# Attention on one core: negated maxima, 1/8 in the keys' copy, the queries' split off GpSimd, V^T P^T in two bursts

## The chip, the cores and the metric

The kernel runs on one core of a Trainium2 chip. A core has a matrix engine (TensorE, in the profile PE, its weight loads apart as PEld), VectorE (DVE), ScalarE (ACT), GpSimd (POOL) and SyncE (SP), which only issues transfers. The metric is the device time of one execution in microseconds (us). Before the change the median of 3 runs is 1202.78 us (1196.05 to 1207.08).

## What is computed

Attention over 4 batches of 8 heads (576 queries and keys of 64 numbers each, with gates `s` that add up along the keys, causal), then a mixture of 8 experts with two experts a token, then a gated layer:

```python
scores = scale * np.matmul(q, k.transpose(0, 1, 3, 2))          # scale = 1/8
cum = np.cumsum(np.maximum(s, 0.0), axis=-1)
bias = -(cum[:, :, :, None] - cum[:, :, None, :])
scores = np.where(causal, -1000000000.0, scores + np.minimum(bias, 0.0))
scores = scores - np.max(scores, axis=-1, keepdims=True)
attn = np.exp(scores)
attn = attn / (np.sum(attn, axis=-1, keepdims=True) + 1e-09)
x = np.matmul(attn, v)                                          # per head
...                                                             # per token, over its two experts of 8:
out[mask] += top2_w[mask, k, None] * (np.maximum(x[mask] @ w1[e], 0.0) @ w2[e])
...
return (1.0 / (1.0 + np.exp(-(x @ w_gate))) * (x @ w_val)) @ w_out
```

## The kernel before

The change touches attention only, which lies at 12 to 262 us of the program; behind it come the experts (L164 to L260) and the last layer (L490 to L561).

**Tiles and steps.** The 32 heads are handled as 16 pairs, p = 0 to 15; four pairs make a batch. A pair's 576 queries are cut into five tiles of 128 (tile 4 holds the last 64 of both heads), taken in the order of `ORD`, (0, 4, 3, 1, 2). Each (pair, tile) is one step, n = 5p + 0..4, 80 in all. All engines execute their instructions in the order in which the program is written (a manual schedule), and the loop at L1005 to L1026 writes it, step by step: the parts of V^T P^T due at that step (`pre`, from the table `AVS`), then the scores of the step, then its row maxima, then the turned probabilities P^T of the step before last (between its banks the things that `todo` lists for the step), then the exponentials, then what `post` and the rest of `todo` list. `advance` lays in the routing of a finished batch, one instruction or a few at a time.

**Operands.** Scores are computed in two float32r parts: `split(p)` makes them for pair p. A load brings queries `qr` and keys `kr` with the same 64 rows twice over the 128 partitions. Of the queries, `qs` is a rounded copy in all 128 rows (L613 on GpSimd) whose second 64 rows are then replaced by the rest, `qr - qs` (the low part, L628 on GpSimd). For the keys, `kk` is the rounded copy (L611 on ScalarE) and `k2` the low part, a head at a time (L628 on VectorE). `q2` is a copy of the queries' high part by a transfer that SyncE issues (L648). Rows 64 to 67 of `q2` and `k2` hold the cumulative gates, which `sums` makes once, eightfold. For pair 0 all of this stands at the start, with the queries' copy on ScalarE. For pair p the generator `split` is advanced at step 5p - 5 (a piece at its end) and at the three steps after.

**Scores to probabilities.** `scores` (L713 to L715, tile 4: L720 to L723) writes a PSUM tile `sc` of two banks, of which there are two, so the scores of step n + 2 wait for the exponentials of step n. `rowmax` finds the maxima (reductions L732, L735) and multiplies them by -1/8 (L733, L736). `softmax` computes exp(sc / 8 + nm) on ScalarE (L751, L754), and `turn` transposes by PE (L771) into one of three banks, copied out by ScalarE (L611; the end of tile 4 by VectorE, L781).

**V^T P^T.** `av(p, j)` adds key tile j's part for both heads (L800); j = None is all of the first 128 queries', copied by VectorE (L803); after j = 4 ScalarE copies the other 448 (L611). `AVS` lists the steps counted from the pair's first, and the parts that come ahead of that step's scores:

```python
AVS = ((8, (None, 0)), (9, (1,)), (10, (2,)), (11, (3, 4)))
```

**Routing.** Six steps behind a batch its tokens are turned (L825), their logits computed (L840, L848) and routed by a chain of small instructions, most on VectorE (`gate`, L863 to L939), with GpSimd scattering the tokens' rows (L943, L944), five steps of the generator between two tiles of tokens. The last batch's routing runs beside the first expert. At steps 68 to 73 the first expert's first three blocks of weights are split too (copy on ScalarE L145, low part on GpSimd L146).

Of the kernel before, what the change touches and what calls it, by code (L numbers as in the profile page):

```python
# [61 lines left out]
def attn_moe_moe2_kernel(ctx: ExitStack, tc: tile.TileContext, q, k, v, s, wgn, noise, wcat, w2cat, out):  # L62
# [51 lines left out]
    def count():  # L114
        """How many tiles of slots each expert needs beyond those of the static schedule, and the most of any"""
# [23 lines left out]
def weights(nc, stage, pool, wcat, e, f, name="w", lo=None):  # L139
    """A block of an expert's weights in two float32r parts; yields between its load and the rest"""  # L140
# [9 lines left out]
def moe(tc, pools, res, gates, stage, ring, W, late, count, xs, ys, wcat, w2cat, w2d, identf, identr):  # L150
    """The experts; returns the tiles of the second layer's weights, of which the last are still to be loaded, and
    its first tokens with their pool. The first expert's first slots come ahead of the rest, beside the routing of
    the last batch, which leaves them alone."""
    nc = tc.nc
    wa = []
    with pools as ctx:
# [10 lines left out]
        # the last expert's first tiles come first: they have the tokens of the second layer's first tiles  # L167
# [100 lines left out]
        def convert(f, g, half=FF2 // 2):  # L268
            """Half a block of the second layer's weights, from the words of its doubles to two float32r parts"""
# [8 lines left out]
            # the exponent's range becomes float32's  # L278
# [49 lines left out]
        def after(j):  # L328
            """The second layer's first tokens, beside the last expert's last tiles, which have none of them"""
# [87 lines left out]
def owners(nc, pool, e, x, n):  # L417
    """Each slot's row of ys and its weight"""
# [63 lines left out]
def fetch(nc, pool, ys, t, reads):  # L482
    """Both outputs of a tile of tokens"""
# [5 lines left out]
def fetch_sum(nc, pool, ys, t):  # L489
    """The sum of both outputs of a tile of tokens"""  # L490
# [7 lines left out]
def feed(nc, y, p, ident, hi, lo):  # L498
    """Tokens turned and in two float32r parts; yields where an instruction waits for the last one"""
# [87 lines left out]
def attention(tc, gates, ahead, q, k, v, s, wgn, noise, aux, xs, identf, identb, mask, ltri, ones, iota_d, carry, valid, wgt, nz, tok):  # L587
    nc = tc.nc
    with ExitStack() as ctx:
# [19 lines left out]
        def same(eng, dst, src):  # L609
            if eng is nc.scalar:  # L610
# [476 lines left out]
```

## Time and profile before

| | before |
|---|---|
| median of 3 runs | 1202.78 us |
| lowest, highest | 1196.05, 1207.08 us |
| span of the profiled execution | 1208.2 us |
| PE busy | 1148.6 us (95%) |
| DVE busy | 609.1 us (50%) |
| ACT busy | 434.5 us (36%) |
| POOL busy | 333.2 us (28%) |
| granted TensorE clock, mean | 0.988 |

The profile is of one execution, 1208.2 us long; times of single instructions come from it. The shares are means over very different stages: attention, where all four engines work, takes the first fifth, and from 262 us on the experts and the last layer keep PE busy. The granted clock is given as a share of its full 2.4 GHz.

### The profile page before, as it was taken

To read this page: it belongs to the slowest core of one execution; us is meant where nothing else is said; L and a number is where in the kernel's file an instruction comes from. 1 tells how busy PE (TensorE), PEld (TensorE's weight loads), DVE (VectorE), ACT (ScalarE), POOL (GpSimd) and SP (SyncE) were. 2 spreads that over 40 slices of the span, in tenths; PEclk is the share of its full clock that TensorE was granted. 3 is DMA by queue.
4 is the path that set the end of the run, shared out by engine and by line. 5 is a ranking of instruction groups with operands and counts; after the bars stand their busy time and mean duration, and the time that the engine had idled before them with its cause. 6 is when DMAs were issued, how large, how long until landed. Compare 5 with 4: busy or idle time off the path is not lost. (4 is left out here: it accounts for less than half of the span.)

```text
span 1208.2 us, 17057 instructions
## 1 busy us (share of the span) xinstructions
PE 1148.6 (95%) x6612; PEld 996.2 (82%) x6612; DVE 609.1 (50%) x1081; ACT 434.5 (36%) x908; POOL 333.2 (28%) x298
## 2 busy tenths in 40 slices
PE   5999789879999999999999998999999999999998
PEld 4566455558999888989888898999999999999997
DVE  6778776835467987889983213121121212212211
ACT  5777556622434333434343323122121211212111
POOL 4331743514234435344535445000000000000000
PEclk9999989989999999999999999999999999999999
DMA  6897646234743645676755343903002030030000
GB/s 220 285 310 239 193 145 190 60 111 151 231 142 102 237 148 199 220 246 211 273 187 192 111 142 113 383 2 79 1 21 58 1 79 1 1 78 1 27 1 27
DMA packets 53100, 163.56 MB, mean 135 GB/s; under 512 B 6894, under 2 KB 7470, under 8 KB 52112
## 3 DMA queue, kind: packets, MB, share of 16 engines
q1 hardware_dynamic: 43552, 128.30, 32.2%
q0 software_dynamic: 9312, 33.90, 8.5%
q8 instruction: 54, 0.88, 0.3%
q14 instruction: 38, 0.31, 0.1%
q10 hardware_dynamic: 144, 0.16, 0.0%
HBM read 111.47 MB, written 46.92 MB: 131 GB/s over the span
## 5 line engine op out<-in xcount | busy, mean ns | idle before, releaser
L146 POOL TENSOR_TENSOR w<-wraw,w 128x1024 fp32r<-128x1024 f32 x62 | 153.1, 2476 | 234.5 <-ACT w L145 230.2
L538 DVE TENSOR_TENSOR sg<-h,sg 128x384 f32<-128x384 f32 x72 | 40.2, 558 | 303.0 <-PE h L535 294.3
L219 PE MATMUL h<-xh,w 128*128 128x320 f32 (+2 forms) x512 | 162.2, 317 | 4.2 <-DVE hl L223 4.2
L221 PE MATMUL h<-xh,w 128*128 128x320 f32 (+2 forms) x512 | 158.7, 310 | 0.0
L220 PE MATMUL h<-xl,w 128*128 128x320 f32 (+2 forms) x512 | 158.5, 310 | 0.0
L233 PE MATMUL y<-w,hh 128*128 128x512 f32 x320 | 126.5, 395 | 0.0
L234 PE MATMUL y<-w,hh 128*128 128x512 f32 x320 | 126.3, 395 | 0.0
L235 PE MATMUL y<-w,hl 128*128 128x512 f32 x320 | 126.1, 394 | 0.0
L533 PE MATMUL h<-xh,wc 128*128 128x384 f32 x336 | 114.0, 339 | 0.0
L535 PE MATMUL h<-xh,wc 128*128 128x384 f32 x336 | 113.0, 336 | 0.0
L534 PE MATMUL h<-xl,wc 128*128 128x384 f32 x336 | 112.9, 336 | 0.0
L145 ACT ACTIVATE w<-wraw 128x1024 fp32r<-128x1024 f32 x68 | 72.0, 1058 | 100.9 <-PE y L235 72.3
L219 PEld LDWEIGHTS h<-xh,w 128*128 128x128 f32 x512 | 96.6, 189 | 8.4 <-DVE hl L223 6.7
L223 DVE SCALAR_TENSOR_TENSOR hl<-h,hh 128x320 fp32r<-128x320 f32 (+2 forms) x128 | 59.0, 486 | 86.4 <-ACT hh L222 78.3
L537 ACT ACTIVATE sg<-h 128x384 f32<-128x384 f32 x72 | 35.5, 493 | 185.1 <-PE h L535 185.1
L220 PEld LDWEIGHTS h<-xl,w 128*128 128x128 f32 x512 | 96.6, 189 | 1.6
L221 PEld LDWEIGHTS h<-xh,w 128*128 128x128 f32 x512 | 96.5, 189 | 0.0
L222 ACT ACTIVATE hh<-h 128x320 fp32r<-128x320 f32 (+2 forms) x128 | 54.8, 436 | 112.1 <-PE h L221 107.0
L494 POOL DMA_DIRECT2D y<-ys x15 | 13.3, 965 | 295.7 <-PE h L535 146.8
L540 ACT ACTIVATE gh<-sg 128x384 fp32r<-128x384 f32 x72 | 37.7, 524 | 156.6 <-DVE sg L538 156.6
L533 PE MATMUL h<-xh,wa 128*128 128x384 f32 x240 | 80.9, 337 | 3.3 <-ACTq L436 3.3
L535 PE MATMUL h<-xh,wa 128*128 128x384 f32 x240 | 80.8, 337 | 0.0
(206 smaller groups left out, 2514.8 us busy)
## 6 DMA issues: line engine op xcount, KB each, us to landing
wraw<-in_wcat_dram SPq DMA_DIRECT2D x68, 512.0 KB
dw<-in_w2cat_dram SPq DMA_DIRECT2D x24, 768.0 KB
w2d<-cw SPq DMA_DIRECT2D x14, 768.0 KB
wc<-w2d POOLq DMA_DIRECT2D x7, 1536.0 KB
xs<-zt SPq DMA_DIRECT2D x40, 258.0 KB
xr<-xs SPq DMA_DIRECT2D x40, 258.0 KB
qr<-in_q_dram SPq DMA_DIRECT2D x16, 640.0 KB
kr<-in_k_dram SPq DMA_DIRECT2D x16, 576.0 KB
```

The source lines that it names most:

```text
L145: nc.scalar.activation(w[:, 0], r, AF.Copy)
L146: (lo or nc.gpsimd).tensor_tensor(w[:, 1], r, f32(w[:, 0]), op=OP.subtract)
L219: nc.tensor.matmul(p, w[:, 0, k], xh[:, c, c0], start=c == 0, stop=False)
L220: nc.tensor.matmul(p, w[:, 0, k], xl[:, c, c0], start=False, stop=False)
L221: nc.tensor.matmul(p, w[:, 1, k], xh[:, c, c0], start=False, stop=c == 3)
L223: nc.vector.scalar_tensor_tensor(hl[:, c0], p, 0.0, f32(hh[:, c0]), op0=OP.max, op1=OP.subtract)
L233: nc.tensor.matmul(y, hh[:, k], w[:, 0, 512:], start=n % FB == 0, stop=False)
L234: nc.tensor.matmul(y, hh[:, k], w[:, 1, 512:], start=False, stop=False)
L235: nc.tensor.matmul(y, hl[:, k], w[:, 0, 512:], start=False, stop=n % FB == FB - 1)
L533: nc.tensor.matmul(q, w[:, 0, s], xh[:, c], start=c == 0, stop=False)
L534: nc.tensor.matmul(q, w[:, 0, s], xl[:, c], start=False, stop=False)
L535: nc.tensor.matmul(q, w[:, 1, s], xh[:, c], start=False, stop=c == 3)
```

## The change

Four things, all in attention.

**Maxima.** The reduction writes its result negated; the multiplications L733 and L736 are left out. **Scale.** 1/8 goes into ScalarE's copy of the keys, so the keys' low part becomes `kr / 8 - kk` in one instruction; the exponentials have no scale, the cumulative gates aren't eightfold any more, and the mask's number is -1e9 instead of -8e9. **Queries' split.** `qs` is copied by ScalarE in one instruction, and the low part computed by VectorE in two, one a head. The pieces of `split` move: the transfer to `q2` is issued behind the first piece, and each step from 5p - 3 on takes two pieces. **V^T P^T.** The parts come in two bursts a pair, at steps 8 and 10.

```diff
-NEG = -8.0e9
+NEG = -1.0e9
-AVS = ((8, (None, 0)), (9, (1,)), (10, (2,)), (11, (3, 4)))
+AVS = ((8, (None, 0, 1)), (10, (2, 3, 4)))
...
-        def same(eng, dst, src):
...
+        def same(dst, src, scale=1.0):
+            nc.scalar.activation(dst, src, AF.Copy, scale=scale)
...
-            def low(eng, dst, src, hi):
-                eng.tensor_tensor(dst, src, f32(hi), op=OP.subtract)
+            def low_q(h):
+                nc.vector.tensor_tensor(qs[64:128, h], qr[64:128, h], f32(qs[64:128, h]), op=OP.subtract)
+
+            def low_k(h):
+                nc.vector.scalar_tensor_tensor(k2[0:64, h, 0:S], kr[0:64, h], ISCALE, f32(kk[0:64, h]), op0=OP.mult,
+                                               op1=OP.subtract)
...
-            same(pool, qs, qr)
-            low(pool, qs[64:128], qr[64:128], qs[64:128])
-            yield
-            same(act, kk, kr)
+            same(qs, qr)
             yield
             nc.sync.dma_start(f32(q2[0:64]), f32(qs[0:64]))
+            same(kk, kr, ISCALE)
+            yield
             for h in range(2):
-                low(dve, k2[0:64, h, 0:S], kr[0:64, h], kk[0:64, h])
+                low_q(h)
                 yield
+                low_k(h)
+                yield
...
-            nc.vector.tensor_scalar(sr, sr, 0.0, 8.0, op0=OP.max, op1=OP.mult)
+            nc.vector.tensor_scalar(sr, sr, 0.0, None, op0=OP.max)
...
-                nc.vector.tensor_reduce(mx, sc[:, :, 0:w], axis=AX.X, op=OP.max)
-                nc.vector.tensor_scalar(nm, mx, -ISCALE, None, op0=OP.mult)
+                nc.vector.tensor_reduce(nm, sc[:, :, 0:w], axis=AX.X, op=OP.max, negate=True)
...
                     nc.scalar.activation(pt[:, h * w:(h + 1) * w], sc[:, h, 0:w], AF.Exp, bias=nm[:, h:h + 1],
-                                         scale=ISCALE, accum_out=SUM[b][:, i, 2 * pp + h:2 * pp + h + 1])
+                                         accum_out=SUM[b][:, i, 2 * pp + h:2 * pp + h + 1])
...
             for i in range(1, 4):
                 at(n + i, next, SP[p], None)
+                if i > 1:
+                    at(n + i, next, SP[p], None)
```

How it stands on ScalarE, from the exponentials of a pair's last tile (128x384) to those of the next pair's second (128x576; `pt<-sc` are exponentials, `pT<-tp` copies of P^T, `ot<-av` the copy of V^T P^T). Before:

```order
L751 ACTIVATE pt,sums<-sc,nm 128x384 x2
L611 ACTIVATE pT<-tp 128x2x2x128
L751 ACTIVATE pt,sums<-sc,nm 128x128 x2
L611 ACTIVATE kk<-kr 128x1152
L611 ACTIVATE ot<-av 128x448
L611 ACTIVATE pT<-tp 128x3x128 x2
L754 ACTIVATE pt,sumt<-sc,nm 128x576
```

And now, in the same place of a pair:

```order
L747 ACTIVATE pt,sums<-sc,nm 128x384 x2
L610 ACTIVATE ot<-av 128x448
L610 ACTIVATE pT<-tp 128x2x2x128
L610 ACTIVATE qs<-qr 128x1280
L747 ACTIVATE pt,sums<-sc,nm 128x128 x2
L610 ACTIVATE kk<-kr 128x1152
L610 ACTIVATE pT<-tp 128x3x128 x2
L750 ACTIVATE pt,sumt<-sc,nm 128x576
```

The queries' copy (`qs<-qr`) is new, ahead of the exponentials of the pair's first tile (128x128), and the copy of V^T P^T has moved from behind the keys' copy to the front.

On VectorE, from the reduction of a pair's second tile (tile 4, 128x1) to the fourth's (`qk` holds the low parts of the keys). Before:

```order
L735 TENSOR_REDUCE mx<-sc 128x1
L736 TENSOR_SCALAR nm<-mx 128x1
L628 TENSOR_TENSOR qk_786<-kr,kk 64x576
L732 TENSOR_REDUCE mx<-sc 128x2
L733 TENSOR_SCALAR nm<-mx 128x2
L628 TENSOR_TENSOR qk_786<-kr,kk 64x576
L803 COPY ot<-tp 128x128
L732 TENSOR_REDUCE mx<-sc 128x2
L733 TENSOR_SCALAR nm<-mx 128x2
L781 COPY pT<-tp 64x2x64
```

And now:

```order
L732 TENSOR_REDUCE nm<-sc 128x1
L622 TENSOR_TENSOR qs<-qr,qs 64x640
L730 TENSOR_REDUCE nm<-sc 128x2
L625 SCALAR_TENSOR_TENSOR qk_753<-kr,kk 64x576
L622 TENSOR_TENSOR qs<-qr,qs 64x640
L799 COPY ot<-tp 128x128
L730 TENSOR_REDUCE nm<-sc 128x2
L625 SCALAR_TENSOR_TENSOR qk_753<-kr,kk 64x576
L777 COPY pT<-tp 64x2x64
```

The small multiplications are gone, two low parts of queries (`qs<-qr,qs`) have come in, and each low part of the keys stands one reduction later.

On PE, at the end of a pair's V^T P^T (`av<-pT,vr`), beside the first and second tile's scores of the pair two further on (`sc`, 128x128 and 128x288). Before, the last burst stands behind the first tile's scores (128x128) and the transposes:

```order
L713 MATMUL sc<-kk,qs 128x128
L714 MATMUL sc<-qk_332 128x128
L715 LDWEIGHTS identb
L715 MATMUL sc<-mask,identb 128x128
L771 MATMUL tp<-identf,pt 128x128 x4
L800 MATMUL av<-pT,vr 64x192 x2
L800 MATMUL av<-pT,vr 64x64 x2
L720 MATMUL sc<-kk,qs 128x288
```

And now it stands, with the third key tile's part, ahead of the first tile's scores:

```order
L796 MATMUL av<-pT,vr 64x320 x2
L796 MATMUL av<-pT,vr 64x192 x2
L796 MATMUL av<-pT,vr 64x64 x2
L712 MATMUL sc<-kk,qs 128x128
L713 MATMUL sc<-qk_321 128x128
L714 LDWEIGHTS identb
L714 MATMUL sc<-mask,identb 128x128
```

The last two key tiles' parts (64x192, 64x64) have moved past the first tile's scores and the transposes; the second tile's scores follow the transposes directly.

## Rows read from the trace of the kernel before

**Rows 1.** Engines by stretch: start:end and length in us, busy us, clock, DMA share.

```profile
core 0: us, PE busy (x) PEld busy (x) DVE busy (x) ACT busy (x) POOL busy (x), PEclk, DMA share, GB/s
15.54:78.16 62.62, 59.39 (x382) 40.34 (x383) 42.13 (x70) 47.24 (x130) 25.89 (x13) 1.00 0.92 295
78.16:109.48 31.32, 27.77 (x209) 18.05 (x208) 28.02 (x70) 20.89 (x60) 8.46 (x5) 1.00 0.86 276
109.48:121.09 11.61, 11.61 (x90) 7.63 (x89) 7.84 (x28) 10.07 (x28) 0.00 (x0) 1.00 0.58 203
121.09:134.78 13.69, 12.00 (x89) 7.95 (x88) 8.64 (x15) 10.22 (x29) 10.81 (x12) 1.00 0.55 161
134.78:174.53 39.75, 31.00 (x210) 19.47 (x209) 32.20 (x82) 20.63 (x58) 20.00 (x20) 0.88 0.50 167
174.53:201.82 27.29, 25.11 (x166) 16.18 (x166) 16.34 (x29) 17.86 (x52) 16.91 (x21) 0.92 0.69 216
201.82:236.37 34.55, 29.51 (x215) 19.15 (x214) 31.63 (x82) 23.27 (x63) 11.81 (x7) 0.95 0.23 61
262.00:1208.00 946.00, 929.01 (x5126) 852.18 (x5126) 423.41 (x669) 268.12 (x459) 222.74 (x182) 1.00 0.35 117
```

**Rows 2.** Instructions by line and shape, 60:240 us: count, busy us, mean ns, idle before.

```profile
L628 POOL TENSOR_TENSOR qs<-qr,qs 64x1280 fp32r<-64x1280 f32 x11 | 32.0, 2910 | 6.2 <-DMA xs<-xt,posi 5.0 <-POOL qs L613 0.6
...
L628 DVE TENSOR_TENSOR qk<-kr,kk 64x576 fp32r<-64x576 f32 x22 | 22.0, 998 | 1.1 <-ACT kk L611 0.6 <-DMA xs<-zt 0.3
L733 DVE TENSOR_SCALAR nm<-mx 128x2 f32<-128x2 f32 x47 | 20.7, 441 | 2.0
...
L146 POOL TENSOR_TENSOR w<-wraw,w 128x1024 fp32r<-128x1024 f32 x3 | 7.2, 2408 | 9.6 <-ACT w L145 5.3 <-issue 4.3
```

**Rows 3.** Timeline 123:131: start us, duration us, engine, instruction, idle before it.

```profile
124.18 0.17 DVE L733 TENSOR_SCALAR nm<-mx 128x2 f32<-128x2 f32 x1
124.26 0.74 DVE L628 TENSOR_TENSOR qk<-kr,kk 64x576 fp32r<-64x576 f32 x1
...
127.97 2.89 POOL L628 TENSOR_TENSOR qs<-qr,qs 64x1280 fp32r<-64x1280 f32 x1 [0.75 <-DMA xs<-xt,posi]
128.69 2.20 DVE L733 TENSOR_SCALAR nm<-mx 128x2 f32<-128x2 f32 x1
...
130.98 0.58 ACT L751 ACTIVATE pt<-sc,nm 128x384 f32<-128x384 f32 x1 [1.76 <-DVE nm L733]
```

**Rows 4.** Waits 134.78:236.37: who waited for what, us in total, times, longest.

```profile
PE sc L713 <- ACT pt L751: 5.1, 2, 3.6
...
PE tp L913 <- DVE ohb L907: 2.8, 1, 2.8
```

**Rows 5.** Timeline 140:171, a scatter and the logits behind it.

```profile
140.25 0.90 POOL L944 DMA_INDIRECT xs<-xt,posi  x1 [0.22 <-issue]
...
141.63 1.19 PE L840 MATMUL tp<-ot,wgt 128*32 128x288 f32 x8 [4.51 <-issue]
```

**Rows 6.** Engines by stretch, the stretch of the lowest granted clock.

```profile
169.00:178.00 9.00, 8.35 (x41) 6.10 (x41) 4.00 (x22) 5.61 (x15) 4.92 (x9) 0.50 0.31 114
```

**Rows 7.** Timeline 118:122, within the ordinary pair.

```profile
118.92 0.81 PE L800 MATMUL av<-pT,vr 128*64 128x192 f32 x8
...
119.66 0.40 PE L720 MATMUL sc<-kk,qs 128*128 128x288 f32 x1
...
120.21 1.17 ACT L611 ACTIVATE kk<-kr 128x1152 fp32r<-128x1152 f32 x1
...
121.49 0.48 PE L713 MATMUL sc<-kk,qs 128*128 128x512 f32 x1
```

**Rows 8.** Timeline 5:12.5, the split of pair 0 at the start.

```profile
7.44 1.25 ACT L611 ACTIVATE qs<-qr 128x1280 fp32r<-128x1280 f32 x1
...
8.73 1.56 DVE L628 TENSOR_TENSOR qs<-qr,qs 64x640 fp32r<-64x640 f32 x2 [0.17 <-ACT qs L611]
```

**Rows 9.** VectorE's instructions by line and shape, 300:750, second layer's weights.

```profile
L292 DVE TENSOR_TENSOR cv<-cv,cu 128x768 f32<-128x768 f32 x24 | 29.2, 1217 | 0.6
L289 DVE SCALAR_TENSOR_TENSOR cv<-dw,ca 128x768 f32<-128x768 uint32 x24 | 24.2, 1008 | 0.7
```

More of the change, by code (lines that the diff above doesn't have):

```diff
@@ L607, in load @@
             raw[p] = (qr, kr, vr)
-        def same(eng, dst, src):
-            if eng is nc.scalar:
-                eng.activation(dst, src, AF.Copy)
-            elif eng is nc.gpsimd:
-                eng.tensor_scalar(dst, src, 1.0, 1.0, op0=OP.mult, op1=OP.mult)
-            else:
-                eng.tensor_copy(dst, src)
+        def same(dst, src, scale=1.0):
+            nc.scalar.activation(dst, src, AF.Copy, scale=scale)
         def split(p):
@@ L623, in split @@
             kk = wk.tile([128, 2, S], F32R, name="kk")
-            act, dve, pool = nc.scalar, nc.vector, nc.gpsimd
             opd[p] = (qs, q2, kk, k2, vr)
-            def low(eng, dst, src, hi):
-                eng.tensor_tensor(dst, src, f32(hi), op=OP.subtract)
+            def low_q(h):
[3 more added lines that the diff above has]
+                                               op1=OP.subtract)
             if p == 0:
-                same(act, qs, qr)
-                same(act, kk, kr)
+                same(qs, qr)
+                same(kk, kr, ISCALE)
                 for h in range(2):
-                    same(act, q2[0:64, h], f32(qs[0:64, h]))
+                    same(q2[0:64, h], f32(qs[0:64, h]))
                 for h in range(2):
-                    low(dve, qs[64:128, h], qr[64:128, h], qs[64:128, h])
+                    low_q(h)
                 for h in range(2):
-                    low((dve, pool)[h], k2[0:64, h, 0:S], kr[0:64, h], kk[0:64, h])
+                    low_k(h)
                 return
@@ L642, in split @@
                 nc.sync.dma_start(f32(k2[64:68, :, 0:S]), aux[:, 1, :, p, 0:S])
-            same(pool, qs, qr)
-            low(pool, qs[64:128], qr[64:128], qs[64:128])
-            yield
-            same(act, kk, kr)
+            same(qs, qr)
             yield
             nc.sync.dma_start(f32(q2[0:64]), f32(qs[0:64]))
+            same(kk, kr, ISCALE)
+            yield
             for h in range(2):
-                low(dve, k2[0:64, h, 0:S], kr[0:64, h], kk[0:64, h])
+                low_q(h)
+                yield
+                low_k(h)
                 yield
@@ L728, in rowmax @@
             w = (i + 1) * 128
-            mx = wk2.tile([128, 2], F32, name="mx", bufs=4)
             nm = wk2.tile([128, 2], F32, name="nm", bufs=4)
             if i < 4:
-                nc.vector.tensor_reduce(mx, sc[:, :, 0:w], axis=AX.X, op=OP.max)
-                nc.vector.tensor_scalar(nm, mx, -ISCALE, None, op0=OP.mult)
-            else:
-                nc.vector.tensor_reduce(mx[:, 0:1], sc[:, :, 0:288], axis=AX.XY, op=OP.max)
-                nc.vector.tensor_scalar(nm[:, 0:1], mx[:, 0:1], -ISCALE, None, op0=OP.mult)
+                nc.vector.tensor_reduce(nm, sc[:, :, 0:w], axis=AX.X, op=OP.max, negate=True)
+            else:
+                nc.vector.tensor_reduce(nm[:, 0:1], sc[:, :, 0:288], axis=AX.XY, op=OP.max, negate=True)
             NM[p, i] = nm
@@ L751, in softmax @@
                     nc.scalar.activation(pt[:, h * w:(h + 1) * w], sc[:, h, 0:w], AF.Exp, bias=nm[:, h:h + 1],
-                                         scale=ISCALE, accum_out=SUM[b][:, i, 2 * pp + h:2 * pp + h + 1])
+                                         accum_out=SUM[b][:, i, 2 * pp + h:2 * pp + h + 1])
             else:
                 nc.scalar.activation(pt[:, 0:S].rearrange("p (c w) -> p c w", c=2), sc[:, :, 0:288], AF.Exp,
-                                     bias=nm[:, 0:1], scale=ISCALE, accum_out=SUMT[b][:, pp:pp + 1])
+                                     bias=nm[:, 0:1], accum_out=SUMT[b][:, pp:pp + 1])
             P[p, i] = pt
@@ L773, in turn @@
                 if i < 2:
-                    same(nc.scalar, pT[:, :, 0:i + 1, q0], t.rearrange("p (h j w) -> p h j w", h=2, w=128))
+                    same(pT[:, :, 0:i + 1, q0], t.rearrange("p (h j w) -> p h j w", h=2, w=128))
                 elif i < 4:
-                    same(nc.scalar, pT[:, g // m, 0:i + 1, q0], t.rearrange("p (j w) -> p j w", w=128))
+                    same(pT[:, g // m, 0:i + 1, q0], t.rearrange("p (j w) -> p j w", w=128))
                 elif g == 0:
-                    same(nc.scalar, pT[:, :, :, q0].rearrange("p h j w -> p j h w"),
+                    same(pT[:, :, :, q0].rearrange("p h j w -> p j h w"),
                          t.rearrange("p (j h w) -> p j h w", h=2, w=64))
@@ L804, in av @@
             elif last:
-                same(nc.scalar, OT[b][:, pp, 128:S], a[:, 0:448])
+                same(OT[b][:, pp, 128:S], a[:, 0:448])
                 opd.pop(p)
```

## The prediction

> **What bounds the kernel now.** I read the granted clock and the span first, then the page's busy shares, then a table of the engines by stretch, then the waits and single pairs. The kernel has two parts. From 262 us on TensorE (PE) is busy 929.01 of 946.00 us (the last row of [rows 1]); the change touches no instruction there, so I cost it at nothing. What can move is attention with its routing, 15 to 236 us.
>
> The other rows of [rows 1] cut that part at the reductions of the pairs' second tiles. Two kinds of pair stand in them. The ordinary pair, 109.48 to 121.09, takes 11.61 us and PE is busy for all of it: PE sets its length. VectorE (DVE) has 7.84 and ScalarE (ACT) 10.07 us in it, GpSimd (POOL) nothing. In the next pair, with POOL busy for 10.81 us (the queries' split and first scatters), PE stands idle for 1.69 us; in the three stretches in which a batch is routed for 3.55, 8.75 and 5.04. Over 15.54 to 236.37 the idle time is 3.23 + 3.55 + 0 + 1.69 + 8.75 + 2.18 + 5.04 = 24.4 us. This is the pool out of which a gain must come.
>
> Who fills it? [Rows 2] has the longer half of POOL's split, 11 low parts of 2.91 us. Beside it stand DVE's small instructions, which should cost little: 47 negations of two numbers a row take 441 ns on average. [Rows 3] shows why. A negation takes 0.17 us and a low part of the keys 0.74 us undisturbed; but the negation that begins at 128.69, while POOL's low part (127.97, 2.89 us) runs, takes 2.20 and ends at 130.89, within 0.03 us of POOL's end at 130.86. ScalarE's exponential then starts at 130.98, having waited 1.76 us. So a DVE instruction that reads SBUF is held until the GpSimd instruction ends. Over 60 to 240 us that is (441 - 170 ns) x 47 = 12.7 us in the negations and (998 - 740 ns) x 22 = 5.7 us in the keys' low parts [rows 2].
>
> **What the change takes off.** It removes every negation (the maximum comes negated from the reduction, which I cost at no more than the reduction now) and the queries' split from POOL. With the split gone, the holds go that came from it, and with the negations the victims of them.
>
> Not all of the 24.4 us is of this kind. The wait of 4.51 us at the logits (L840), which ends at 141.63, has no releaser in the profile and ends only when a scatter of POOL's does, at 141.15 [rows 5]; POOL issues its scatters there one behind another, and these stay. The exponential for which PE waits 3.6 us at 228 [rows 4] is late behind the first expert's weights on POOL (L146, three low parts of 2.41 us in [rows 2]), which stay too. Left: 24.4 - 4.5 - 3.6 = 16.3, of which I take 15; the rest is for waits too small to trace.
>
> Something comes back by the clock. PE waits once 2.8 us for a mask of the routing's from DVE (L907) [rows 4]; behind that, from 169 to 178, the granted clock is 0.50, the lower of the two levels (1.2 of 2.4 GHz) [rows 6]. That wait ends a chain of small DVE instructions which were held in turn; if it shrinks, the 8.35 us of PE work there may run in half the time: 4 us. Gross gain 15 + 4 = **19 us**.
>
> V^T P^T in two bursts takes off two joins between other work and 64-row matmuls, a pair. Here is no row of a join by itself. Lower bound: nothing, since PE has the same matmuls. Upper: at 118.92 eight of them take until 119.66 [rows 7], 0.09 each; a join can't be worth more than one, so 0.18 a pair, 2.9 us over 16 pairs. I take 0.1 a pair: **1.6 us**.
>
> **What it adds.** (1) ScalarE gets the copy of the queries. At the start it is there already: 1.25 us [rows 8]. It now stands between the copy of P^T and the exponentials of the pair's first tile. (2) The second burst (0.74 us, 118.92 to 119.66 in [rows 7]) goes ahead of that tile's scores instead of behind them, so its maximum comes 0.74 later. [Rows 7] gives the effect on an ordinary pair: the exponentials of the first tile end where the keys' copy starts, at 120.21. With both delays that is 120.21 + 0.74 + 1.25 = 122.20. PE starts the third tile's scores at 121.49, and they go into the two banks that those exponentials read. PE's own work up to there is the same in sum, since the burst only changes sides, so PE waits 122.20 - 121.49 = 0.7 us. Times 15 pairs: **10.5 us**. Its bounds: 0.3 a pair if ScalarE starts the queries' copy earlier in a gap (it has 11.61 - 10.07 = 1.54 us idle a pair [rows 1]); 0.74 + 1.25 = 1.99 a pair if no idle time is left and ScalarE becomes the chain (10.07 + 1.25 = 11.32 of 11.61). I take 0.7, as the row gives it.
>
> (3) DVE gets two low parts of queries a pair, 0.78 us each (two in 1.56 in [rows 8]), and loses four negations of 0.17 and one shorter: +0.8 net. 7.84 + 0.8 = 8.6 of 11.61 us; PE's work hides it in an ordinary pair. In the routing stretches DVE is busy 28.02 of 31.32, 32.20 of 39.75 and 31.63 of 34.55 [rows 1], but that busy time contains the holds; with those gone (18.4 us in all) the additions (13 pairs' worth, 10 us) find room. So nothing for it there, at most 5 us over the three. (4) The keys' low part becomes a scale and a subtraction in one. [Rows 9] has both forms on 128x768 in the second layer: 1008 ns with a scalar, 1217 without. The form costs nothing more. (5) The factor 1/8 in the keys' copy, and the exponential without a scale: instructions of the same shapes, 0. (6) The copies of queries to the other operand (SP) wait for ScalarE now and not for POOL, and stand ahead of the zeros: earlier by the 2.91 us of POOL's low part, hidden before and after by five steps. The keys' low parts come one step later; the next load of keys waits for them. That load has a pair of time; hidden. (7) POOL's scatters, no longer broken up by a split between them, may run ten in a row; PE's late signals happen only inside such runs. From 0 to the 4.5 us of another such wait [rows 5]; I take **1.5 us**.
>
> **Sum.** -19 - 1.6 + 10.5 + 1.5 = -8.6, say -9 us. The profiled execution took 1208.2 us, 5.4 above the median of the runs (1202.78). So its span would be about 1199 us, and the median 1202.78 - 9 = **1194 us**.
>
> **Rivals.**
> A, the other side: ScalarE becomes the bound. It is at 10.07 of 11.61 us and gets 1.25. If the delays chain from pair to pair, each costs 1.99: 15 x 1.99 = 30 instead of 10.5, and the sum is -19 - 1.6 + 30 + 1.5 = +11: 1214 us. It is slower as soon as a pair loses over (19 + 1.6 - 1.5) / 15 = 1.3 us. For it: ScalarE's order is fixed, and PE's next scores wait for it. Against: 11.32 is still under 11.61. Chance 0.12.
> B: the gain is eaten. If the routing's chains are late for other reasons than POOL (dependent small DVE instructions, which stay) half of the 19 us stays, and the rest pays for ScalarE: -9.5 - 1.6 + 10.5 + 1.5 = +1: about 1203. For it: each routing stretch keeps its own 28 to 32 us of DVE. Chance 0.2.
> C: ScalarE's copy fits into its idle time (0.3 a pair, 4.5): -19 - 1.6 + 4.5 + 0 = -16, and -20 where a low-clock stretch more comes back (134.78 to 174.53 is granted 0.88 on average, [rows 1]): 1183 us. Chance 0.14.
> D: the keys' low parts in the new form take twice as long, +0.74 each, 1.5 a pair. In ordinary pairs DVE then has 10.1 of 11.61 and hides it; in six pairs of routing it lies on the chain: +9, so 1203 us. [Rows 9] speaks against it (the form with a scalar was the shorter), so 0.03. The Trainium skill ("Vector Engine (DVE) Microarchitecture Reference", section "Points that are easy to get wrong") has a rule of this kind: an operation of a scalar and two tensors runs at half its rate when both tensors lie in SBUF and aren't bf16. By that rule D would be the forecast; this trace disagrees, its 1008 ns instruction has two 32-bit sources in SBUF.
>
> **How the numbers follow.** The forecast has 0.51, with a range of its own from 1187 to 1201 (a pair's cost 0.3 to 1.0). The predicted time is its time, 1194 us. A reaches from 1203 to 1214 and above, B from 1198 to 1207, C from 1178 to 1188. 1182 to 1208 leaves out about half of C (0.07) and most of A (0.1). About 1% is what a measurement of this kernel can tell from no change. Faster by more (below 1190.8): C and 0.45 of the forecast, 0.37. Slower by more (above 1214.8): half of A and a little beside it, 0.08. The rest, 0.55, is within 1%.
>
> **What would show it.** Right: no DVE instruction ends with a POOL split any more, and those of 0.17 us are gone; the two low parts of queries take 0.78 us each; PE waits some 0.7 us a pair at the third tile's scores for an exponential; the low clock from 169 us is gone or shorter; the waits inside scatter bursts and behind L146 remain. Wrong: PE's wait per pair is near 2 us and follows ScalarE throughout (A); PE's idle time in the three routing stretches is as before (B); ordinary pairs still take 11.6 us (C); the keys' low parts take 1.4 us (D). Holds of DVE that remain with POOL idle would refute the reading of [rows 3].

## The result, and the profile after

The changed kernel takes 1187.58 us in the median of four runs (1185.98 to 1189.42), the kernel before 1201.18 on the same occasion: a ratio of 0.9894 (95% interval 0.9858 to 0.993), 1.1% less. Beside undisturbed runs of the kernel before (experiments 5 and 6) the medians are 9.9 us apart, a ratio of 0.9919 (0.9902 to 0.9935). The forecast was 1194 us, 9 us or 0.7% less; the range held it. That it came out so near is in part luck: terms of its sum were wrong in opposite directions, as the experiments show.

The two profiled executions are 1208.2 and 1187.5 us long, 20.7 apart, where the medians are 13.6 apart: the trace of before contains disturbances that the trace of after has not, and that don't belong to the change (waits at 141 and 251 us, told of at the end as late signals). First the table of the engines by stretch of the changed kernel, cut as [rows 1] at the reductions of second tiles (columns as there):

```profile
core 0: us, PE busy (x) PEld busy (x) DVE busy (x) ACT busy (x) POOL busy (x), PEclk, DMA share, GB/s
...
77.95:107.36 29.41, 26.89 (x209) 18.30 (x208) 25.15 (x63) 22.07 (x60) 0.00 (x0) 1.00 0.84 277
...
119.34:131.07 11.73, 11.00 (x84) 7.67 (x83) 7.51 (x11) 10.80 (x29) 8.95 (x18) 1.00 0.89 289
131.07:160.50 29.43, 26.96 (x215) 18.49 (x214) 26.38 (x75) 22.09 (x60) 0.08 (x1) 1.00 0.47 160
...
184.07:219.75 35.68, 29.83 (x215) 20.57 (x214) 32.51 (x77) 24.99 (x66) 7.15 (x4) 0.90 0.27 80
```

The stretch of the second batch's routing (131.07 to 160.50) has PE busy for 26.96 of 29.43 us at a full clock, where the corresponding row of [rows 1] had 31.00 of 39.75 at 0.88 (4.51 us of its idle time were a late signal). Behind attention nothing moved: from the reduction of the last pair's second tile to the end, experiments 5 and 6 take 967.2 and 966.1 us. The third batch's routing (184.07 to 219.75) keeps its waits and its low clock. An ordinary pair, 119.34 to 131.07, takes 11.73 us, about what it took before (11.61 in [rows 1], 11.80 where the split runs beside it), but in another way: PE works 11.00 us of it and waits 0.73. By the prediction's terms it would have grown to 11.61 + 0.7 - 0.1 = 12.2 us.

Groups by line and shape of the changed kernel, 60 to 240 us (busy us, mean ns behind the first bar):

```profile
L622 DVE TENSOR_TENSOR qs<-qr,qs 64x640 fp32r<-64x640 f32 x23 | 18.9, 822 | 0.6
L625 DVE SCALAR_TENSOR_TENSOR qk<-kr,kk 64x576 fp32r<-64x576 f32 x23 | 17.2, 746 | 0.3
L610 ACT ACTIVATE qs<-qr 128x1280 fp32r<-128x1280 f32 x11 | 14.0, 1268 | 0.0
```

The low parts of queries take 0.82 us (0.78 was expected), the copy 1.27 (1.25), and the keys' low parts are back at 0.75 us in their new form, against 998 ns in [rows 2] and 0.74 us undisturbed in [rows 3]: nothing holds them any more, and scale and subtraction in one cost nothing.

The wait of PE is the one that the prediction named, for the exponentials of the pair's first tile; this is the line of the table of waits, 15 to 262 us (total, times, longest):

```profile
PE sc L712 <- ACT pt L747: 13.9, 14, 3.9
```

Ten of the 14 are of 0.71 to 0.74 us, one a pair at its third tile's scores; the longest, 3.93, stands behind the first expert's weights.

### The profile page after: what moved, and what is told of

Same layout as the page of the kernel before. It is cut to its first block, busy times and chain, and to the rows that moved or that the text cites. A ratio compares the mean times of both kernels' runs of the same rounds, so it can differ in the third digit from the quotient of the medians.

```text
span 1187.5 us, 16987 instructions
## 1 busy us (share of the span) xinstructions
PE 1138.0 (96%) x6612; PEld 997.6 (84%) x6612; DVE 593.7 (50%) x1032; ACT 450.3 (38%) x923; POOL 268.1 (23%) x267
## 5 line engine op out<-in xcount | busy, mean ns | idle before, releaser
L146 POOL TENSOR_TENSOR w<-wraw,w 128x1024 fp32r<-128x1024 f32 x62 | 153.3, 2479 | 253.4 <-ACT w L145 253.2
L534 PE MATMUL h<-xl,wa 128*128 128x384 f32 x240 | 81.9, 341 | 0.0
```

Source lines behind the costliest of these rows:

```text
L146: (lo or nc.gpsimd).tensor_tensor(w[:, 1], r, f32(w[:, 0]), op=OP.subtract)
L534: nc.tensor.matmul(q, w[:, 0, s], xl[:, c], start=False, stop=False)
```

## The experiments

The twelve runs (1 to 4, 5 to 8, 9 to 12) came in three groups, each with its own runs of the kernel before (medians 1214.0, 1198.4 and 1211.7 us); the first two ran on the same chip, the third on another. Times are compared as ratios to before within a group. In the first and third group every trace shows the disturbances told of at the end ("late signals"); in the second none does. So the clean sizes are read from pairs in which no such wait stands, and from the second group. The kernel after ran only in the second, so its time is compared with none of the first and third.

**1. Four bursts.** The kernel after, with

```diff
-AVS = ((8, (None, 0, 1)), (10, (2, 3, 4)))
+AVS = ((8, (None, 0)), (9, (1,)), (10, (2,)), (11, (3, 4)))
```

> The kernel after, with V^T P^T in four bursts a pair as before. Theory J (a burst more costs PE about 0.3 us at its start and end): PE's own work in an ordinary pair rises from 11.0 to about 11.64 us, but the first tile's exponentials come 0.74 earlier, so the wait of 0.73 us at the third tile's scores goes; ordinary pairs take 11.6 to 11.7 instead of 11.73 to 11.76, and the time is within 2 us of the kernel after (1187.6). Theory P (as predicted, a burst costs 0.05 us): pairs of 11.1 us, the time 7 to 9 us lower, near 1179.

Measured: 1216.08 us, 1.0014 of before (0.9985 to 1.0043). Ordinary pairs take 11.94 us, of which PE is busy 11.71:

```profile
66.41:78.35 11.94, 11.71 (x85) 7.62 (x83) 7.60 (x11) 10.85 (x29) 0.00 (x0) 1.00 1.01 315
```

The wait at the third tile is gone and the work is back, 0.7 us of it (11.00 to 11.71). So the work that theory J gives a burst is there; P, by which pairs would have been 11.1, falls. J's pairs of 11.6 to 11.7 us didn't come, nor its time: PE waits another 0.23 us a pair for ScalarE's copies of P^T. That the whole gain is gone here isn't the bursts alone: PE's waits by late signals, 3.8 to 5.9 us each, stand in this trace. How much of it is the bursts these times don't show.

**2. Copy late.** The kernel after, the queries' copy behind the first tile's exponentials:

```diff
             same(qs, qr)
-            yield
             nc.sync.dma_start(f32(q2[0:64]), f32(qs[0:64]))
...
-            at(n, next, SP[p])
             post[n] = SP[p]
```

> The kernel after, with the queries' copy on ScalarE moved behind the exponentials of the pair's first tile. Theory W (the copy ahead of the exponentials costs 0.73 us a pair): the wait of PE at the third tile's scores is gone, ordinary pairs take 11.0 us instead of 11.73 to 11.76, some 7 us less in ten pairs: 1180. Rival A (ScalarE is the chain, with 10.8 busy of 11.73 us a pair): the wait turns up at a later tile's scores, pairs take 11.5 us or more, the time 1185 or above.

Measured: 1203.11 us, 0.9938 of before (0.9911 to 0.9966), pairs of 11.76 us. The wait did turn up elsewhere, as rival A had it. From the timelines of PE and ScalarE in one pair:

```profile
65.57 1.17 ACT L610 ACTIVATE kk<-kr 128x1152 fp32r<-128x1152 f32 x1
66.62 0.87 ACT L610 ACTIVATE pT<-tp 128x384 f32<-128x384 f32 x2
...
67.17 0.44 PE L795 MATMUL tp<-pT,vr 128*64 128x128 f32 x4 [0.79 <-ACT pT L610]
```

The queries' and the keys' copy now stand one behind the other, and the copies of P^T behind both; V^T P^T waits 0.79 us for them. But ScalarE isn't full: it is 10.7 us busy a pair. That leaves its order, which experiment 7 tests.

**3 and 11. Two bursts alone.** The kernel before, with only the table `AVS` of after; run in the first and the third group.

> The kernel before, with V^T P^T in two bursts a pair, nothing else changed. Theory J: some 0.6 us a pair less on PE in ordinary pairs (11.6 becomes 11.0 to 11.1, since the later scores of the first tile cost next to nothing as long as ScalarE has no copy of queries), 6 to 9 us in all: 1192 to 1195. Theory P: 1.6 us in all, not to be told from 1201.

> The kernel before with two bursts alone, once more, in one session with the runs beside it. Theory J: ordinary pairs 11.05 to 11.1 us instead of 11.8, and 7 to 9 us less than before where no late signals disturb it (0.6 to 0.75%).

Measured: 0.9968 (0.9945 to 0.999) and 0.9944 (0.9925 to 0.9963) of before. Ordinary pairs fall from 11.80 to 11.07 us, the same in both traces (the row of experiment 11, of the table by stretch):

```profile
64.04:75.11 11.07, 11.04 (x84) 7.68 (x83) 7.13 (x14) 9.83 (x28) 4.17 (x2) 1.00 1.03 337
```

So the two bursts are worth 0.7 us an ordinary pair, with the queries' split still on GpSimd (4.17 us of POOL in that pair). The prediction had put 0.1. In time they are worth 4.5 us (1.2 to 6.7) and 5.9 us (4.5 to 9.1), less than the 6 to 9 and 7 to 9 that were expected: in the pairs of routing nothing is won, the first batch's take 17.85 and 14.0 to 14.1 us where before has 17.26 and 14.1.

**4. Split off alone.** The kernel before, with

```diff
-            same(pool, qs, qr)
-            low(pool, qs[64:128], qr[64:128], qs[64:128])
+            same(act, qs, qr)
...
+                low(dve, qs[64:128, h], qr[64:128, h], qs[64:128, h])
+                yield
                 low(dve, k2[0:64, h, 0:S], kr[0:64, h], kk[0:64, h])
...
+                if i > 1:
+                    at(n + i, next, SP[p], None)
```

(The transfer to `q2` moves ahead of the keys' copy, and pair 0 has both low parts of keys on VectorE, as in the kernel after.)

> The kernel before, with the queries' split alone off GpSimd (copy on ScalarE, low parts on VectorE, placed as in the kernel after); multiplications by -1/8, scales and four bursts stay. If the split on GpSimd is what held VectorE: the multiplications take 0.17 us throughout, the routing pairs fall to about 17.1 us, and the time is that of the kernel after with four bursts (within 3 us). If the negated maxima or the 1/8 in the keys' copy have a worth of their own: 5 us or more above it.

Measured: 1216.06 us, 1.0018 of before (0.9996 to 1.0039), the same as experiment 1. The negations are hardly held any more:

```profile
L734 DVE TENSOR_SCALAR nm<-mx 128x2 f32<-128x2 f32 x46 | 9.7, 211 | 2.0
```

211 ns against 441 in [rows 2]; where the remaining 40 above 170 come from wasn't followed. The first routing pair takes 16.26 us (17.26 before), an ordinary pair 11.94 (11.80 before). Once the split is off GpSimd, leaving out the negations on top (experiment 1) is worth nothing that these times show.

**5 and 6. Before and after again**, in the second group.

> The kernel before once more, for a trace from the same chip as the runs beside it. Theory L (PE's signals come late inside a run of scatters, and a low clock follows, more on one chip than on another): waits of 3 to 6 us without a running instruction behind them in two or three of the batches' scatters, and 0.50 of clock behind each. If such waits were chance of the one profile, they are missing here or stand elsewhere.

> The kernel after once more, beside the others on one chip. Ordinary pairs 11.73 to 11.76 us with a wait of 0.73 at the third tile's scores. If its gain on the first chip came from the missing late signals, here, where they stand in every kernel tried so far, it is only that of the two bursts less the wait: 0.2 to 0.5%; otherwise 1% again.

Measured: before 1200.28 us in the profiled run, its group's median 1198.43; after 1188.55, a ratio of 0.9919 (0.9902 to 0.9935). Late signals were expected in both traces, and there are none, on the chip on which all of the first group had them. The same ordinary pair in both, before first:

```profile
64.39:76.19 11.80, 11.64 (x84) 7.58 (x83) 7.70 (x14) 9.81 (x28) 4.16 (x2) 1.00 1.00 325
```

```profile
65.12:76.88 11.76, 11.03 (x85) 7.73 (x84) 7.51 (x11) 10.80 (x29) 0.00 (x0) 1.00 1.03 324
```

PE's work falls by 0.61 us, a wait of 0.73 comes in, the pair keeps its length. The two traces are 1198.5 and 1184.5 us long; this pair of undisturbed traces is what the terms are sized by below. They lie 14.0 us apart, the medians 9.9: one is of the slowest run of before in its group, the other of the fastest of after.

**7. Copies spread.** The kernel after, the queries' copy behind the first tile's exponentials, the keys' copy behind those of the third:

```diff
             same(qs, qr)
-            yield
             nc.sync.dma_start(f32(q2[0:64]), f32(qs[0:64]))
-            same(kk, kr, ISCALE)
             yield
             for h in range(2):
                 low_q(h)
                 yield
+            same(kk, kr, ISCALE)
+            yield
+            for h in range(2):
                 low_k(h)
                 yield
...
-            at(n, next, SP[p])
-            post[n] = SP[p]
-            for i in range(1, 4):
+            post[n] = post[n + 2] = SP[p]
+            for i in (1, 2, 3, 3):
                 at(n + i, next, SP[p], None)
-                if i > 1:
-                    at(n + i, next, SP[p], None)
```

> The kernel after with ScalarE's two copies spread: the queries' behind the exponentials of the pair's first tile, the keys' two steps later, behind the exponentials of the third; the keys' low parts both at the fourth step. Theory W: no wait is left in an ordinary pair, which takes 11.0 to 11.1 us instead of 11.75; 7 us less than the kernel after on the same chip. Rival A (ScalarE is the chain): 11.4 or more, under 3 us.

Measured: 1180.58 us, 0.9854 of before (0.9837 to 0.987), 8.0 us less than the kernel after beside it. An ordinary pair:

```profile
64.17:75.49 11.32, 11.12 (x84) 7.62 (x83) 7.52 (x11) 10.63 (x30) 0.00 (x0) 1.00 1.04 320
```

11.32 us, between the two expectations: PE's wait is down to 0.2 us, and ScalarE with 10.63 us busy doesn't set the pair. So what the change lost to ScalarE was its order, for the larger part; this version beats both kernels.

**8. Scatters paced.** The kernel after, each scatter of the first two batches behind the row maxima of a step (`nc.gpsimd.tensor_copy(spacer, LAST[0][0:1, 0:1])` in place of the `memset` of `spacer`, and four pieces of the routing between two scatters).

> The kernel after with the scatters of the first two batches paced: each waits for the row maxima of a step (about 2.4 us apart) instead of running one behind another every 1.28 us; those of the third batch are as they were. Theory L: the late signals in the first two runs of scatters are gone, the one at the third remains, and the time falls by what they and their low clock cost, 8 to 15 us against the kernel after on a chip that has them, nothing on one that has not. Rival: each scatter or the traffic of its rows makes them late, paced or not: no change.

Measured: 1187.95 us, 0.9905 of before, as the kernel after. But its group had no late signals, so it tells nothing of them. That pacing costs nothing is all that it shows.

**9. Split back on GpSimd.** The kernel after, with negated maxima, 1/8 and two bursts, but

```diff
-            same(qs, qr)
+            nc.gpsimd.tensor_scalar(qs, qr, 1.0, 1.0, op0=OP.mult, op1=OP.mult)
+            nc.gpsimd.tensor_tensor(qs[64:128], qr[64:128], f32(qs[64:128]), op=OP.subtract)
             yield
-            nc.sync.dma_start(f32(q2[0:64]), f32(qs[0:64]))
             same(kk, kr, ISCALE)
             yield
+            nc.sync.dma_start(f32(q2[0:64]), f32(qs[0:64]))
             for h in range(2):
-                low_q(h)
-                yield
                 low_k(h)
                 yield
...
-                if i > 1:
-                    at(n + i, next, SP[p], None)
```

> The kernel after with the queries' split back on GpSimd (copy and one low part of 64x1280), and the pieces of the split at the steps of the kernel before; negated maxima, 1/8 in the keys and two bursts stay. ScalarE has no copy of queries, so the wait of 0.73 us in ordinary pairs goes: 11.05 us instead of 11.76, 7 us less in ten pairs. Theory H (GpSimd's split holds VectorE, and PE pays for it in the batches' routing): the routing pairs lose 8 to 12 us again (waits of 2 to 3 us behind held instructions of the routing, the low clock behind them), the time is that of the kernel after or 5 us above. If the negations were the victims that mattered: routing pairs as in the kernel after, some 7 us below it.

Measured: 1196.96 us where before took 1211.65: 0.9867 (0.9839 to 0.9896), the best ratio of its group and 8.8 us below experiment 11, which differs from it by the negations and the scale (and, at the start, by one low part of pair 0); the scale alone wasn't tried. An ordinary pair and the first routing pair of its table by stretch:

```profile
60.65:71.39 10.74, 10.74 (x85) 7.59 (x84) 5.77 (x9) 9.65 (x30) 4.17 (x2) 1.00 1.03 318
71.39:87.35 15.96, 15.52 (x128) 10.74 (x127) 14.40 (x32) 11.11 (x32) 4.16 (x2) 1.00 1.03 353
```

10.74 us with GpSimd busy for 4.17 of them and PE idle for none; the routing pair 15.96, where the kernel after has 17.08 (77.95 to 95.03). Yet the holds are there, from its groups by line:

```profile
L625 DVE SCALAR_TENSOR_TENSOR qk<-kr,kk 64x576 fp32r<-64x576 f32 x22 | 22.8, 1035 | 4.9 <-ACT kk L610 4.1 <-DMA vr<-in_v_dram 0.4 <-DMA qk<-aux 0.4
```

1035 ns against 746: 6.4 us of holds over 22 instructions, and in these two pairs PE pays next to nothing (15.52 of 15.96 us busy in the second). In the second batch's routing it still does: an instruction of the chain (L895, 0.2 us when free) ends with GpSimd's low part of 154.75 to 157.64, and PE waits for the mask behind it:

```profile
155.79 1.90 DVE L895 TENSOR_TENSOR g<-iota_d,m 128x40 f32<-128x40 f32 x1
...
158.22 0.20 PE L908 MATMUL tp<-ohb,ltri 128*128 128x48 bf16 x1 [1.82 <-DVE ohb L902]
```

Theory H falls in its strong form. The negations were the victims that mattered, since an exponential waited for each; the keys' low parts can be late. Once the negations are gone, the split does better on GpSimd than on ScalarE and VectorE as the kernel after has it, in the pairs ahead of the first scatters. Behind them this trace has late signals, and there it isn't shown.

**10. Weights' low parts on VectorE.** Experiment 7, with `lo=nc.vector` for the first expert's first three blocks (L146).

> The kernel with the spread copies, and the low parts of the first expert's first three blocks on VectorE instead of GpSimd (L146). Theory H: the routing's instructions L877 and L879 take 0.2 us instead of 2.3, the wait of PE of 3.9 to 4.4 us at 204 to 211 us shrinks below 1.5, and the low clock behind it goes: 3 to 6 us less than the spread copies alone. Rival: VectorE's own three low parts, over 1.2 us each, take their place in the chain: within 2 us.

Measured: 1200.17 us, 0.9898 of before (0.9869 to 0.9928), in the third group. The held instructions take 0.20 us again, but PE's wait stays:

```profile
207.82 1.23 DVE L146 TENSOR_TENSOR w<-wraw,w 128x1024 fp32r<-128x1024 f32 x1 [1.69 <-ACT w L145]
...
210.15 0.74 ACT L751 ACTIVATE pt<-sc,nm 128x576 f32<-128x576 f32 x1 [1.60 <-DVE nm L733]
...
216.26 0.69 PE L713 MATMUL sc<-kk,qs 128*128 128x384 f32 x1 [3.70 <-ACT pt L748]
```

VectorE now waits 1.69 us for ScalarE's copy of the weights and computes for 1.23, with a reduction behind it in its order, and the exponential behind that; a second low part at 211.96 stands ahead of the next reduction in the same way, whose exponential PE waits for at 216.26. The rival was right as to the wait: 3.70 us against 4.42 in experiment 7. The time of experiment 7 comes from another group, so the two aren't compared.

**12. Four bursts again.**

> The kernel after with four bursts a pair, once more, in one session with the runs beside it. Ordinary pairs 11.94 us as in its first trace; the routing pairs those of the kernel after, with another 0.6 us for the joins. Where no late signals disturb it the time is 2 to 4 us above the kernel after, so 0.5 to 0.7% below before: what holds and negations alone are worth.

Measured: 1210.39 us, 0.9985 of before (0.9966 to 1.0003); ordinary pairs of 11.94 us as in experiment 1. The 0.5 to 0.7% that were expected without late signals can't be read here, since the trace has four waits of 2.4 to 5.7 us of that kind or behind the weights. Against experiment 9 of the same group it is 1.1% slower.

**The same five pairs in all traces.** All groups can be compared in one stretch: from the reduction of the third pair's second tile to that of the eighth's, three ordinary pairs and the two beside the first batch's routing. No trace has a scatter or a late signal in it, and the granted clock is 1.00 in all. Traces of the same kernel agree within 0.06 us in it (before 67.13 and 67.19, experiments 3 and 11 65.54 and 65.49, after 64.67 and 64.68).

| kernel (experiment) | from, to | length | PE busy |
|---|---|---|---|
| before (5) | 40.39, 107.58 | 67.19 us | 63.03 us |
| before, two bursts (11) | 41.48, 106.97 | 65.49 us | 60.71 us |
| before, split moved (4) | 42.25, 107.47 | 65.22 us | 63.00 us |
| after, four bursts (12) | 42.23, 106.56 | 64.33 us | 62.83 us |
| after (6) | 41.61, 106.29 | 64.68 us | 59.95 us |
| after, copies spread (7) | 41.52, 104.12 | 62.60 us | 60.04 us |
| after, split back (9) | 39.17, 98.93 | 59.76 us | 58.89 us |

The parts don't add up, each depends on the others. Two bursts alone take off 1.7 us; on top of the rest of the change they add 0.4, since the wait for ScalarE comes with them. Leaving out the negations (with the scale) takes off 5.7 where the split holds them, 0.9 where it is gone. Moving the split takes off 2.0 by itself and adds 4.9 where the negations are gone already. The whole change takes off 2.5 here; most of its gain lies behind these pairs, where the second and third batch are routed and GpSimd scatters: from there to the last pair's reduction experiment 5 takes 123.7 us, experiment 6 112.1.

## Why the prediction was nearly right, point by point

The undisturbed traces (experiments 5 and 6) differ by 1198.5 - 1184.5 = 14.0 us, the medians of their group by 9.9. Predicted were 9. The terms are read from the two traces, so none is known better than the 4 us between these figures.

**The bursts: 1.6 predicted; 9.8 of PE's work saved (0.61 us by 16 pairs), of time alone 4.5 and 5.9** (experiments 3 and 11). The step that failed is "Upper: ... a join can't be worth more than one" matmul. The trace of before had the price of a join in it, in rows that I hadn't read as one. PE in the ordinary pair of before (109 to 121.5 us), a lone burst and the transposes ahead of each:

```profile
111.43 0.44 PE L800 MATMUL tp<-pT,vr 128*64 128x128 f32 x4
...
112.55 0.39 PE L713 MATMUL sc<-kk,qs 128*128 128x256 f32 x1
...
113.33 0.72 PE L771 MATMUL tp<-identf,pt 128*128 128x128 f32 x5
113.98 0.97 PE L800 MATMUL av<-pT,vr 128*64 128x448 f32 x4
114.88 0.44 PE L713 MATMUL sc<-kk,qs 128*128 128x384 f32 x1
...
117.04 0.76 PE L800 MATMUL av<-pT,vr 128*64 128x320 f32 x4
117.73 0.33 PE L713 MATMUL sc<-kk,qs 128*128 128x128 f32 x1
...
118.38 0.61 PE L771 MATMUL tp<-identf,pt 128*128 128x128 f32 x4
```

And the weight loads at the start of the lone burst:

```profile
113.98 0.20 PEld L800 LDWEIGHTS av<-pT,vr 128*64 128x64 f32 x4 [0.20 <-issue]
```

The same work in the kernel after:

```profile
122.22 0.44 PE L796 MATMUL tp<-pT,vr 128*64 128x128 f32 x4
122.49 1.70 PE L796 MATMUL av<-pT,vr 128*64 128x448 f32 x8
124.12 0.39 PE L712 MATMUL sc<-kk,qs 128*128 128x256 f32 x1
...
124.90 0.71 PE L767 MATMUL tp<-identf,pt 128*128 128x128 f32 x5
125.37 0.42 PE L712 MATMUL sc<-kk,qs 128*128 128x384 f32 x1
...
127.33 1.35 PE L796 MATMUL av<-pT,vr 128*64 128x320 f32 x12
128.60 0.33 PE L712 MATMUL sc<-kk,qs 128*128 128x128 f32 x1
...
129.25 0.61 PE L767 MATMUL tp<-identf,pt 128*128 128x128 f32 x4
129.61 0.38 PE L719 MATMUL sc<-kk,qs 128*128 128x288 f32 x1
```

Read from start to start. Five transposes ahead of a burst take 113.98 - 113.33 = 0.65 us, ahead of scores 125.37 - 124.90 = 0.47; four of them 118.92 - 118.38 = 0.54 [rows 7] and 129.61 - 129.25 = 0.36. So a burst's start costs 0.18, twice a pair. The bursts themselves took 0.90 at 113.98, 0.69 at 117.04, 0.74 at 118.92 [rows 7] and 112.55 - 111.43 = 1.12 for the first; now 124.12 - 122.22 = 1.90 and 128.60 - 127.33 = 1.27: 3.45 against 3.17. Together 0.18 + 0.18 + 0.28 = 0.64 us a pair. A busy share of 100% hid it: the profile counts PE as busy through the join (the five transposes at 113.33 are listed with 0.72 us, longer than the 0.65 to the burst).

**The wait behind ScalarE's copy: 10.5 predicted, 7.3 to 8.0 measured as idle time.** The working from [rows 7] gave 0.7 us and the trace has 0.73; it stands in 10 or 11 of the 15 pairs, since in the rest, the second pair of each routing above all, PE waits for other things. Mechanism and place were right, and the price nearly. (Ordinary pairs near 11.6 us were named as a sign of rival C. They came about with the forecast's wait in them, since the bursts pay for it.) In time it is nearer 1.0 us a pair. Experiment 6, the transposes ahead of the wait and the third tile's scores:

```profile
64.86 0.85 PE L767 MATMUL tp<-identf,pt 128*128 128x128 f32 x6
66.44 0.50 PE L712 MATMUL sc<-kk,qs 128*128 128x512 f32 x1 [0.73 <-ACT pt L747]
```

And experiment 9, without the wait:

```profile
60.39 0.85 PE L766 MATMUL tp<-identf,pt 128*128 128x128 f32 x6
61.00 0.48 PE L711 MATMUL sc<-kk,qs 128*128 128x512 f32 x1
```

From start to start 1.58 against 0.61 us, 0.97 more, of which the profile counts 0.24 as busy. Rival A is refuted by experiment 7: ScalarE's busy time in a pair stays about the same (10.63 us against 10.80), the time falls by 8 us, and the order is what differs.

**The holds: 19 predicted (15 and 4 of clock), about 12 left for them.** What is left of the 14.0 us, 14.0 - 9.8 + 8.0 = 12.2, is for holds, clock and all else: a remainder, not a measurement. It lies mostly in the pairs of routing (for the second batch, 18.41 + 15.64 before and 17.08 + 12.35 after, from the reductions of second tiles in experiments 5 and 6). The size that failed is that of the idle time. From the first to the last pair's reduction PE is idle for 19.2 us in experiment 5 (215.73 long, 196.56 busy), not 24.4, and for 20.7 in experiment 6 (202.27, 181.55), of which 8.0 are the wait for ScalarE: other idle time fell by 6.5 us where 15 was predicted. The mean clock there is 0.96 and 0.98, by an estimate from these some 5 us; that part was about right.

That VectorE is held until the GpSimd instruction ends stays true (2.20 us in [rows 3], 1.90 in experiment 9); but the step "With the split gone, the holds go that came from it, and with the negations the victims of them" counted the two as one thing. Experiment 9 parts them: the negations gone and the split left where it was gives pairs of 10.74 instead of 11.07 us, and routing pairs of 15.96 instead of 17.85 (experiment 11), with the holds still there. Of the change's parts, the move of the split is the one that isn't needed in these pairs: with the negations gone it adds about 1 us a pair (11.76 against 10.74, 17.08 against 15.96). The two versions weren't run in one group, so their difference in time over the whole kernel isn't measured, nor is it known whether the split may stay on GpSimd beside the scatters, where a hold still cost 1.82 us.

**The scatters: 1.5 predicted, nothing measured, and not by the reason given.** The ten scatters do run in a row, and the waits inside them are absent from both undisturbed traces and present in every trace of two groups, whatever the kernel. They don't go with the split: it is off GpSimd in experiments 1, 2, 4, 10 and 12, which have them, and on it in experiment 5, which has none. So the 4.5 us that were left out of the gain as "these stay" didn't stay in the trace of after, and the profile's 20.7 us are some 7 to 11 more than the change is worth (14.0 by the undisturbed traces, 9.9 by the medians). A second such wait, 5.67 us at 251.51, lay behind the stretch that the prediction looked at.

**The weights behind the first expert (3.6 us): stays**, as said. The timeline of after shows the hold with its victims and PE at the end of the chain:

```profile
203.28 4.79 POOL L146 TENSOR_TENSOR w<-wraw,w 128x1024 fp32r<-128x1024 f32 x2 [29.56 <-ACT w L145]
203.49 2.25 DVE L877 TENSOR_TENSOR g<-g,nz 128x40 f32<-128x40 f32 x1
...
205.78 2.35 DVE L879 TENSOR_TENSOR g<-g,lg 128x40 f32<-128x40 f32 x1
...
211.08 0.69 PE L712 MATMUL sc<-kk,qs 128*128 128x384 f32 x1 [3.93 <-ACT pt L747]
```

Two instructions of the routing that take 0.2 us each when free (experiment 10) take 2.25 and 2.35; the reduction for the next exponential stands behind them in VectorE's order. Here a hold does cost, because of what is queued behind it.

**The keys' low part in its new form: nothing, as said** (746 ns). Rival D falls, and with it the rule of the Trainium skill ("Vector Engine (DVE) Microarchitecture Reference", section "Points that are easy to get wrong") as a forecast for this shape: both tensors lie in SBUF and are 32-bit wide, and the instruction isn't slower than the plain subtraction's 0.74 us in [rows 3].

So against the two traces the sum was 5 us short: 8.2 too little for the bursts' work, about 7 too much for the holds, 2.5 to 3 too much for ScalarE's wait, 1.5 for the scatters. Against the medians it was 1 us short. The nearness is luck in so far as the first two nearly cancel; and the sum took the parts as independent, which the five pairs show that they aren't.

## What to carry to other kernels

Read PE's price of a switch from start to start, the transposes ahead of a burst included: a full busy share hides it. A held or late instruction costs only what waits behind it: ask for the victim before moving the cause, since taking away 80 tiny instructions here did more (5.7 us in five pairs) than moving 4 us a pair off the engine that held them (2.0). And where an engine with idle time becomes the one that is waited for, try its order before its load: two copies moved by one and two steps gave back 8 us.

## What wasn't expected of the hardware

**Signals that come late.** In the trace of before and in all eight runs of the first and third group, engines wait for work that the trace shows as done, always while GpSimd issues scatters or a few us behind the last. Experiment 12, timeline of all engines:

```profile
174.91 0.42 PE L712 MATMUL sc<-kk,qs 128*128 128x384 f32 x1
...
175.50 0.66 PE L767 MATMUL tp<-identf,pt 128*128 128x128 f32 x4
...
177.86 0.90 POOL L940 DMA_INDIRECT xs<-xt,posi  x1 [0.22 <-issue]
180.84 0.69 DVE L730 TENSOR_REDUCE nm<-sc 128x2 f32<-128x512 f32 x1 [5.39 <-remote]
180.89 0.60 ACT L610 ACTIVATE pT<-tp 128x512 f32<-128x512 f32 x1 [7.28 <-remote]
181.54 1.11 PE L767 MATMUL tp<-identf,pt 128*128 128x128 f32 x4 [5.39 <-ACT pT L610]
```

The transposes end at 176.16 and the reduction's scores earlier; VectorE and ScalarE start at 180.84 and 180.89. Behind it the granted clock goes to its lower level, and four transposes of the same form take 1.11 us instead of 0.66; the row of the stretch behind it, with a clock of 0.52:

```profile
182.00:194.00 12.00, 12.00 (x55) 8.01 (x55) 4.34 (x8) 8.76 (x23) 0.00 (x0) 0.52 0.52 163
```

In the second group no kernel has them: before takes 1198.4 us there, 1211.7 and 1214.0 in the others. PE's waits of this kind add up to 10.2 us in the trace of before and 13.8 in experiment 1, and the lower clock comes on top. What makes the signals late isn't known. It isn't the chip alone, since the first and the second group ran on the same one; pacing the scatters was tried only where none were late.
